# A decode kernel whose last four weight blocks move from behind TensorE's loop into its body

## The chip, the cores and the metric

The kernel runs on one core of one Trainium2 chip. The metric is the device time of one execution in microseconds. Three runs of the kernel before took 775.5, 776.76 and 776.8 us; their median is 776.76 us.

## The reference

Two branches on the same two rows `x` (2 x 1024) are mixed by a gate:

```python
g = sigmoid((x * gate_w).sum(-1, keepdims=True))
q = (x @ wq)                               # 32 heads of 128, 4 kv heads, 32768 cached positions
a = softmax(q k^T / sqrt(128)) v, heads joined, @ wo      # wo: 4096 x 1024
b = x + gelu(layernorm(x) @ w3) @ w4       # w3: 1024 x 3584, w4: 3584 x 1024
out = g * a + (1 - g) * b
```

The sequence has one position, so the shifted branch through `w1` and `w2` is zero and isn't computed. All data are float32. The keys and values (two caches of 2 x 4 x 32768 x 128) are 268 MB of the 331 MB that are read.

## The kernel before, in words

All large data come through one queue, SP's, in one order: `wq`, `w3`, then for each of the 8 pairs of batch row and kv head two halves of 8 MB of keys and two of values, with `w4` between pair 3 and pair 4 and `wo` behind pair 7. They go into two buffers (`ring`, named `load` in the trace) of 64 KB per partition. A load waits until TensorE has finished with what stood in its buffer (`load`, L196), so that while one half is worked on, the other one is under way.

A "block" of `w4` or `wo` is 128 x 1024 numbers, one per partition row: `w4` has 28 blocks, `wo` 32. The first 28 blocks of either go into the two ring buffers in four pieces of 14, 8, 4 and 2 blocks (`weights`, `STEPS`). The last four blocks of `wo` have a buffer of their own, `tail` (16 KB per partition), filled by three loads: two blocks, one block, one block, with the semaphores `came[4]`, `came[5]` and `came[6]`.

TensorE's program has straight code at its start (projections of `wq` and `w3`), then a loop of two passes (L491). One pass runs four turns of an inner loop (L492, `turn`, one pair each) and then `weigh` (L482), which multiplies the 28 blocks by the columns in `w_pad` and adds them to `acc`: in the first pass the blocks are `w4`'s and the columns the activations, in the second pass `wo`'s and the attention outputs. Behind the loop stands straight code for the last four blocks of `wo`, from `tail`, with columns of their own, `o_pad` (L570 to L573):

```python
for sem, cs in ((came[4], (0, 1)), (came[5], (2,)), (came[6], (3,))):
    pe.after((sem, 16))
    for c in cs:
        last = into_acc(o_wide, c, tail[:, c * D:(c + 1) * D], last=(c == 3))
```

`into_acc` (L346) issues 8 matmuls of 32 columns by 128 per block. A float32 matmul stands in the trace as two records on PE and two weight loads on PEld, so a block is 16 records. `Line.take` (L49) is one instruction on the waiting engine that waits for a semaphore and lowers it again, so that a loop can use the same semaphore in each pass; `Line.after` is a plain wait.

VectorE, behind its own loop, waits for the end of the `w4` pass (`weighed(1)`) and writes the gated attention outputs to `o_pad` and `w_pad` (L565), then releases TensorE's second `weigh`. ScalarE copies `acc` out after `END` and issues the output's DMA. GpSimd clears the padded buffers at the start (L259), and VectorE waits for the last of these before it writes the first padded columns (L290).

Of the kernel before, what the change touches and what calls it, by code (L numbers as in the profile page):

```python
# [15 lines left out]
B, D, HQ, HKV, SK, DH, F = 2, 1024, 32, 4, 32768, 128, 3584  # L16
REP = HQ // HKV
PAIRS = B * HKV
# [4 lines left out]
KF = F // P  # L23
C = 32
# [4 lines left out]
SHIFT = 8  # L29
# [42 lines left out]
def kernel(  # L72
# [47 lines left out]
    nc = tc.nc  # L120
# [5 lines left out]
    def new(name, *shape, parts=P):  # L126
        return sb.tile([parts, *shape], F32, name=name)

    ring = [new(f"load{i}", PART, WIDE) for i in range(2)]
    tail = new("tail", 4 * D)  # L130
# [3 lines left out]
    x_pad = new("x_pad", KD, C)  # L134
    xn_pad = new("xn_pad", KD, C)
    xr_wide = new("xr_pad", SHIFT + KD * C)
    q_pad = new("q_pad", PAIRS + 1, PART, 2, C)
    q_cur = new("q_cur", PART, 2, C)
    o_all = new("o_all", PAIRS, PART, REP)
    o_wide = new("o_pad", SHIFT + 4 * C)  # L140
    w_wide = new("w_pad", SHIFT + KF * C)
    xr_pad, o_pad, w_pad = (t[:, SHIFT:].rearrange("p (k c) -> p k c", c=C) for t in (xr_wide, o_wide, w_wide))
    sel = new("sel", G, REP)
    sel_all = new("sel_all", REP)
    part = new("part", 2 * B)
# [1 line left out]
    gate = new("gate", B)  # L147
# [16 lines left out]
    p = new("p", NI, NT, PART + 1, HALF)  # L164
# [19 lines left out]
    pe, dve, act, pool, sp = (Line(tc, e, n) for e, n in (  # L184
        (nc.tensor, "pe"), (nc.vector, "dve"), (nc.scalar, "act"), (nc.gpsimd, "pool"), (nc.sync, "sp")))
    landed = [tc.alloc_semaphore(f"landed{i}") for i in range(2)]
    came = [tc.alloc_semaphore(f"came{i}") for i in range(7)]
# [8 lines left out]
    def load(dst, src, sem, *marks):  # L196
        sp.after(*marks)
        nc.sync.dma_start(dst, src).then_inc(sem, 16)  # L198

    def run(src, j):  # L200
        return src[PART * j:PART * (j + 1)].rearrange("i (q w) c -> (i q) (w c)", w=PART)
# [5 lines left out]
    PROLOGUE = ("run", "sum", "var", "q0", "q1", "qt", "h0", "h1", "ht")  # L207
    TURN = ("k0", "v0", "v1")
    STEP = ("s0", "s2", "s3", "mt", "bp", "tp00", "tp01", "tp02", "tp03", "tp10", "tp11", "tp12", "tp13", "lp", "op")

    def at(name, m=None):
        if m is None:
            return (pe.sem, 1 + PROLOGUE.index(name))
        return (pe.sem, len(PROLOGUE) + m * len(TURN) + m // 4 * 2 + 1 + TURN.index(name))

    def weighed(i):
        return (pe.sem, len(PROLOGUE) + 4 * len(TURN) + 1 + i)

    END = (pe.sem, len(PROLOGUE) + PAIRS * len(TURN) + 2 * 2 + 1)


    load(flat[0], run(wq, 0), came[0])
    load(flat[1], run(wq, 1), came[1])
    sixteen = nc.sync.to_reg(16)
    load(flat[0][:, :PART * 2 * F], run(w3, 0), came[2], at("q0"))
    load(flat[1][:, :PART * 2 * F], run(w3, 1), came[3], at("q1"))

    half = PART * KF // 4
    STEPS = ((0, 14), (14, 8), (22, 4), (26, 2))

    def weights(src, *free):
        for (lo, n), sem in zip(STEPS, w_in):
            j = lo // half
            piece = slice((lo - j * half) * D, (lo - j * half + n) * D)
            load(flat[j][:, piece], run(src, j)[:, piece], sem, free[j])

    for m in range(PAIRS):
        free = [at("h" + "01"[j]) if m == 0 else at("v" + "01"[j], m - 1) for j in range(2)]
        if m == 4:
            weights(w4, *free)  # L240
            free = [weighed(0), weighed(1)]
        for j in range(2):
            load(flat[j], run(kt[m], j), landed[j], free[j])
        for j in range(2):
            load(flat[j], run(vt[m], j), landed[j], (at("k0", m), (k1_free, m + 1))[j])
    weights(wo, at("v0", PAIRS - 1), at("v1", PAIRS - 1))
    load(tail[:, :2 * D], run(wo, 0)[:, half * D:], came[4])
    for c in range(2):
        load(tail[:, (2 + c) * D:(3 + c) * D], run(wo, 1)[:, (half + c) * D:(half + c + 1) * D], came[5 + c])


    nc.scalar.dma_start(xg_sb, xg).then_inc(got_x, 16)
# [2 lines left out]
    made = pool.mark(nc.gpsimd.affine_select(  # L255
        out=ident, in_=ident, pattern=[[-1, P]], base=0, channel_multiplier=1,
        compare_op=ALU.not_equal, fill=1.0))
    for t in (x_pad, xn_pad, xr_wide, q_pad, o_wide, w_wide):
        zeroed = pool.mark(nc.gpsimd.memset(t, 0.0))  # L259
    d_ones = dve.mark(nc.vector.memset(ones, 1.0))  # L260
    dve.after(made)
# [13 lines left out]
    for i in range(2):  # L275
        last = nc.vector.tensor_copy(perm[:, :, i], ident.rearrange("p (q w) -> p w q", w=PART))
    d_perm = dve.mark(last)

    def over_k(t):
# [5 lines left out]
    d_part = dve.mark(nc.vector.tensor_reduce(  # L285
        part[:, B:2 * B], xs.rearrange("p k b -> p b k"), axis=AX.X, op=ALU.add))
    dve.after(at("run"), zeroed)
    for i in range(2):
        own = slice(i * HALF, (i + 1) * HALF)
        last = nc.vector.tensor_copy(  # L290
            x_run[own].rearrange("p (j w k) b -> p j w (k b)", j=2, w=PART),
            tr[1][own, :PART * KD * B].rearrange("p (w j i k b) -> p i j w (k b)", w=PART, j=2, i=2, b=B)[:, i])
# [21 lines left out]
    for w in range(PART):  # L314
        last = nc.tensor.matmul(tr[1][:, w * KD * B:(w + 1) * KD * B], perm[:, w].rearrange("p i q -> p (i q)"), xs,  # L315
                                start=True, stop=True)
# [25 lines left out]
    def shifted(t, k, i):  # L342
        lo = SHIFT * (1 - i) + k * C
        return t[:, lo:lo + C]

    def into_acc(t, k, rows, last=False):  # L346
        for i in range(2):
            for g in range(G):
                lo = (2 * g + i) * P
                inst = nc.tensor.matmul(acc[C * g:C * g + C], shifted(t, k, i), rows[:, lo:lo + P],  # L350
                                        start=False, stop=(last and i == 1), skip_group_check=True)
        return inst
# [11 lines left out]
    for i in range(2):  # L364
        last = nc.vector.tensor_copy(twice[:, :, :, i], row.rearrange("p u (h q w) -> p (u h) w q", q=HALF, w=PART))
# [3 lines left out]
    for r in range(REP):  # L369
        for w in range(PART):  # L370
            last = nc.tensor.matmul(qt_ps[:, w, r], twice[:, r, w].rearrange("p i q -> p (i q)"), compact,
                                    start=True, stop=True)
    done = pe.mark(last)
    dve.after(done)
    for i in range(2):
        own = slice(i * HALF, (i + 1) * HALF)
        for s in range(2):
            lo = (2 * s + i) * REP
            last = nc.vector.tensor_copy(q_pad[own, :PAIRS, :, s, lo:lo + REP], qt_ps[own].rearrange("p w h m -> p m w h"))
# [15 lines left out]
    n = KF // G  # L395
    both = p.rearrange("p i t w q -> p (i t w q)")[:, :n * P * 2].rearrange("p (c w i q) -> p c w i q", c=n, w=PART, i=2)
    dve.after(d_h, a_h, at("qt"))
    for i in range(2):
        last = nc.vector.tensor_copy(
            both[:, :, :, i], row.rearrange("p u n -> p (u n)")[:, :n * P].rearrange("p (c q w) -> p c w q", q=HALF, w=PART))  # L400
# [3 lines left out]
    for c in range(n):  # L404
        for w in range(PART):
            o = (c * PART + w) * PAIRS
            last = nc.tensor.matmul(ht_ps[:, o:o + PAIRS], both[:, c, w].rearrange("p i q -> p (i q)"), compact,
                                    start=True, stop=True)
# [11 lines left out]
    for i in range(2):  # L420
        for j in range(2):
            own = slice(i * HALF, (i + 1) * HALF)
            last = nc.vector.tensor_mul(
                w_pad[own, j * PART * n:(j + 1) * PART * n, ::C // B].rearrange("p (w c) b -> p w c b", w=PART),
                h[own].rearrange("p (c w j i b) -> p i j w c b", c=n, w=PART, j=2, i=2)[:, i, j],
                rest[own].rearrange("p (o z b) -> p o z b", o=1, z=1).to_broadcast([HALF, PART, n, B]))
# [55 lines left out]
    def weigh():  # L482
        pe.take(x_in)
        for (lo, n), sem in zip(STEPS, w_in):
            pe.take(sem, 16)
            for c in range(lo, lo + n):
                last = into_acc(w_wide, c, flat[c // half][:, c % half * D:(c % half + 1) * D])
            if lo == 0 or lo + n == KF:
                pe.mark(last)

    with nc.tensor.Fori(0, 2, 1):  # L491
        with nc.tensor.Fori(0, PAIRS // 2, 1):  # L492
            turn()
        weigh()
# [22 lines left out]
    with nc.vector.Fori(0, PAIRS, 1) as m:  # L517
        turn_of = Turn(dve, own_step)
        for i in range(NI):
            if i != 1:  # L520
                nc.vector.wait_ge(*seen(f"s{i}"))
                if i == 3:
                    nc.vector.sem_inc(k1_free, 1)
                last = [nc.vector.reduce_max(out=mx[:, k:k + 1], in_=sc[k], axis=AX.X)  # L524
                        for k in ((1, 2) if i == 2 else (i,))][-1]
# [19 lines left out]
        for i in range(2):  # L545
            last = nc.vector.tensor_copy(pv_sb[:, :, :, i], pv.rearrange("p (s q w) -> p s w q", q=HALF, w=PART))  # L546
# [9 lines left out]
        dve.take(step, len(STEP))  # L556


    dve.after(weighed(1))
    o_by_block = o_all.rearrange("p (a i b) w h -> p i a (w h) b", a=2, i=2)  # L560
    for t, lo, n in ((o_pad, half, 2), (w_pad, 0, half)):
        for i in range(2):
            own = slice(i * HALF, (i + 1) * HALF)
            for b in range(B):
                last = nc.vector.tensor_scalar_mul(  # L565
                    t[own, :, b * (C // B)].rearrange("p (j c) -> p j c", j=2), o_by_block[own, i, :, lo:lo + n, b],
                    gate[own, b:b + 1])
    last.then_inc(x_in, 1)

    for sem, cs in ((came[4], (0, 1)), (came[5], (2,)), (came[6], (3,))):  # L570
        pe.after((sem, 16))
        for c in cs:
            last = into_acc(o_wide, c, tail[:, c * D:(c + 1) * D], last=(c == 3))  # L573
    last.then_inc(pe.sem, 1)
    act.after(END)
    a_out = act.mark(nc.scalar.copy(o_sb, acc))  # L576
    act.after(a_out)
# [34 lines left out]
```

## Time and profile before

| what | value |
|---|---|
| median of 3 runs | 776.76 us (775.5 to 776.8) |
| the profiled execution's own time | 777.06 us |
| its span, first to last instruction | 775.3 us |
| busy: PE, PEld, DVE, ACT, POOL | 433.7, 198.0, 94.2, 60.7, 3.4 us |
| DMA | 331.53 MB at a mean of 428 GB/s |
| granted TensorE clock, mean | 0.763 |
| last chain, shares of the span | DMA `tail<-wo` 4%, PE `pv` 1% |

The span covers what the engines did; 1.8 us of the execution's time lie outside of it. The page divides the span into 40 equal slices of 19.4 us and gives for each the busy share of an engine or of the 16 DMA engines in tenths. A matmul's start is measured and its end modelled. "PEq L51" as the releaser of idle time is the wait instruction in `take`, mostly for a load; "issue" is idle time in which the engine waited for nothing that the profile shows. "q8 instruction" among the DMA queues carries instructions, not data.

### The profile page before, as it was taken

How to read it: one execution, taken by the hardware profiler on the slowest of the kernel's cores; microseconds unless marked ns; L12 is line 12 of the kernel's file. 1: busy time of each engine (PE TensorE's matmuls, PEld its weight loads, DVE VectorE, ACT ScalarE, POOL GpSimd, SP SyncE). 2: the span in 40 equal slices, each digit the busy share in tenths (PEclk: the TensorE clock that was granted, in tenths of full speed). 3: DMA queues.
4: the chain of work that ended last, by engine and by line, in shares of the span. 5: the costliest groups of instructions: out<-in, count | busy, mean ns of one | idle time of the engine just before them, and what ended most of it. 6: DMA issues, size and time to landing. Idle time of an engine off the chain costs nothing. (4 is left out here: it accounts for less than half of the span.)

```text
span 775.3 us, 8384 instructions
## 1 busy us (share of the span) xinstructions
PE 433.7 (56%) x3772; PEld 198.0 (26%) x3772; DVE 94.2 (12%) x266; ACT 60.7 (8%) x144; POOL 3.4 (0%) x12
## 2 busy tenths in 40 slices
PE   0564747454746564647466247465646474547475
PEld 0231413221323132213235013131312131213164
DVE  1110202100210021002100002100210021002110
ACT  0000002000200020002000002000200020002000
POOL 1000000000000000000000000000000000000000
PEclk9977676876686688677879567767967787768779
DMA  9999999999999999999999999999999999999996
GB/s 379 433 431 437 436 437 440 430 434 436 440 433 436 436 433 433 433 433 433 429 420 446 433 433 433 433 433 433 433 433 433 433 433 436 433 433 433 424 424 265
DMA packets 6955, 331.53 MB, mean 428 GB/s; under 512 B 913, under 2 KB 929, under 8 KB 1185
## 3 DMA queue, kind: packets, MB, share of 16 engines
q1 hardware_dynamic: 6768, 331.35, 99.0%
q8 instruction: 9, 0.15, 0.1%
q10 hardware_dynamic: 176, 0.02, 0.0%
q14 instruction: 2, 0.01, 0.0%
HBM read 331.36 MB, written 0.01 MB: 427 GB/s over the span
## 5 line engine op out<-in xcount | busy, mean ns | idle before, releaser
L441 PE MATMUL sc<-load,q_cur 128*32 128x512 f32 x1024 | 151.2, 756 | 133.1 <-PEq L51 133.1
L468 PE MATMUL pv<-load,pt 128*32 128x512 f32 x1024 | 131.5, 672 | 89.4 <-PEq L51 89.4
L441 PEld LDWEIGHTS sc<-load,q_cur 128*32 128x32 f32 x1024 | 41.3, 135 | 236.6 <-issue 236.6
L468 PEld LDWEIGHTS pv<-load,pt 128*32 128x32 f32 x1024 | 39.7, 122 | 171.4 <-issue 171.4
L458 PE MATMUL sc<-ident,p 128*128 128x128 f32 x256 | 44.4, 347 | 22.8 <-PEq L51 22.8
L524 DVE TENSOR_REDUCE mx<-sc 128x1 f32<-128x512 f32 x32 | 21.4, 689 | 287.8 <-PE sc L441 287.8
L508 ACT ACT_TABLE_LOAD x8 | 10.3, 1283 | 493.6 <-ACTq L51 493.6
L458 PEld LDWEIGHTS sc<-ident,p 128*128 128x128 f32 x256 | 39.9, 183 | 30.0 <-issue 30.0
L350 PE MATMUL acc<-load,w_pad 128*32 128x128 f32 x896 | 30.3, 299 | 13.9 <-PEq L51 10.3
L541 DVE COPY pt<-sc 64x256 f32<-64x256 f32 x64 | 25.9, 414 | 71.9 <-PE sc L458 71.5
L350 PEld LDWEIGHTS acc<-load,w_pad 128*32 128x32 f32 x896 | 28.3, 122 | 15.6 <-issue 15.6
L514 ACT COPY pt<-sc 64x256 f32<-64x256 f32 x64 | 23.5, 368 | 75.9 <-PE sc L458 73.6
L546 DVE COPY pv_sb<-pv 128x512 f32<-128x512 f32 x16 | 10.3, 685 | 152.9 <-PE tr L474 152.9
L478 PE MATMUL tr<-sel,pv_sb 128*128 128x8 f32 x128 | 20.6, 298 | 11.8 <-PEq L51 11.8
L478 PEld LDWEIGHTS tr<-sel,pv_sb 128*128 128x128 f32 x128 | 20.1, 247 | 12.3 <-issue 12.3
L330 PE MATMUL sc<-load,x_pad 128*32 128x512 f32 x128 | 17.4, 706 | 7.5 <-DMA load<-wq 7.5
L508 ACT ACTIVATE p<-sc,bias 128x512 f32<-128x512 f32 x32 | 21.6, 686 | 0.1
L330 PE MATMUL sc<-load,xn_pad 128*32 128x384 f32 (+1 forms) x128 | 15.1, 631 | 11.3 <-DMA load<-w 11.3
L315 PE MATMUL tr<-xg_sb,perm 128*128 128x16 f32 x4 | 1.0, 372 | 23.4 <-DMA xg_sb<-xg 23.4
L537 DVE COPY p<-p 128x256 f32<-128x256 f32 x32 | 9.4, 294 | 26.7 <-ACT p L508 26.7
L330 PEld LDWEIGHTS sc<-load,xn_pad 128*32 128x32 f32 x128 | 4.2, 126 | 21.9 <-DMA load<-w 12.4
L330 PEld LDWEIGHTS sc<-load,x_pad 128*32 128x32 f32 x128 | 4.3, 128 | 19.8 <-issue 11.3
(83 smaller groups left out, 88.7 us busy)
## 6 DMA issues: line engine op xcount, KB each, us to landing
load<-w SPq DMA_DIRECT2D x3, 7168.0 KB, 26.2
load<-wo SPq DMA_DIRECT2D x1, 7168.0 KB, 28.6
load<-w SPq DMA_DIRECT2D x1, 4096.0 KB, 17.6
load<-wo SPq DMA_DIRECT2D x1, 4096.0 KB, 17.0
load<-w SPq DMA_DIRECT2D x1, 2048.0 KB, 22.2
load<-wo SPq DMA_DIRECT2D x1, 2048.0 KB, 21.6
load<-w SPq DMA_DIRECT2D x1, 1024.0 KB, 24.1
load<-wo SPq DMA_DIRECT2D x1, 1024.0 KB, 23.6
```

The costliest lines, as they stand in the source:

```text
L330: last = nc.tensor.matmul(b[C * g:C * g + C, :hi - lo], pad[:, k], t[:, o + lo:o + hi], start=(k == 0), stop=(k == KD - 1))
L350: inst = nc.tensor.matmul(acc[C * g:C * g + C], shifted(t, k, i), rows[:, lo:lo + P], start=False, stop=(last and i == 1), skip_group_chec ...
L441: last = nc.tensor.matmul(sc[i][C * g:C * g + C], q_cur[:, w, s], ring[j][:, w, o:o + 512], start=(s == 0 and w == 0), stop=(s == 1 and w ...
L458: last = nc.tensor.transpose(sc[k][:, t * P:(t + 1) * P], pair.rearrange("p w q -> p (w q)"), ident)
L468: last = nc.tensor.matmul(pv[C * g:C * g + C], pt[j][w][:, lo:lo + C], ring[j][:, w, o:o + G * DH], start=(j == 0 and w == 0 and t == 0), ...
L478: last = nc.tensor.matmul(tr[1][:, w * REP:(w + 1) * REP], pv_sb[:, s, w].rearrange("p i q -> p (i q)"), sel[:, s], start=(s == 0), stop=( ...
L508: nc.scalar.activation(p[:, i, :, :PART], sc[i].rearrange("p (t q w) -> p t w q", t=NT, w=PART), AF.Exp, bias=bias, scale=scale, accum_out ...
L514: nc.scalar.copy(*halves(1, j, c)).then_inc(pt_in[c], 1)
L524: last = [nc.vector.reduce_max(out=mx[:, k:k + 1], in_=sc[k], axis=AX.X) for k in ((1, 2) if i == 2 else (i,))][-1]
L537: nc.vector.tensor_copy(p[:, i, :, PART], p[:, i, :, 0]).then_inc(p_in[i], 1)
L541: nc.vector.tensor_copy(*halves(0, j, c)).then_inc(pt_in[c], 1)
L546: last = nc.vector.tensor_copy(pv_sb[:, :, :, i], pv.rearrange("p (s q w) -> p s w q", q=HALF, w=PART))
```

## The change

The three parts for `tail` move into `weigh`, and so into the loop's body. They now run in both passes. In the first one they multiply zeros by zeros: GpSimd clears `tail` at the start, and the columns 28 to 31 of `w_pad` stay zero until VectorE writes them after the first pass. `o_pad` goes; `w_pad` grows from 28 to 32 blocks of columns. So that the first pass doesn't wait for loads, VectorE raises the three semaphores by 16 each at the start, and `take` lowers them again. `pe.mark` behind the last block is a third mark per pass (the `* 2` in `at` becomes `* 3`), VectorE waits for this third mark (`weighed(2)`) before it writes `w_pad`, and ScalarE's `END` is the same mark in the second pass.

```diff
-    o_wide = new("o_pad", SHIFT + 4 * C)
-    w_wide = new("w_pad", SHIFT + KF * C)
+    w_wide = new("w_pad", SHIFT + HQ * C)
...
-        return (pe.sem, len(PROLOGUE) + m * len(TURN) + m // 4 * 2 + 1 + TURN.index(name))
+        return (pe.sem, len(PROLOGUE) + m * len(TURN) + m // 4 * 3 + 1 + TURN.index(name))
...
-    END = (pe.sem, len(PROLOGUE) + PAIRS * len(TURN) + 2 * 2 + 1)
+    END = (pe.sem, len(PROLOGUE) + PAIRS * len(TURN) + 2 * 3)
...
-    for t in (x_pad, xn_pad, xr_wide, q_pad, o_wide, w_wide):
+    for t in (x_pad, xn_pad, xr_wide, q_pad, w_wide, tail):
         zeroed = pool.mark(nc.gpsimd.memset(t, 0.0))
...
     dve.after(at("run"), zeroed)
+    for sem in came[4:]:
+        nc.vector.sem_inc(sem, 16)
...
             if lo == 0 or lo + n == KF:
                 pe.mark(last)
+        lo = 0
+        for (_, _, n), sem in zip(rest_of_wo, came[4:]):
+            pe.take(sem, 16)
+            for c in range(lo, lo + n):
+                last = into_acc(w_wide, KF + c, tail[:, c * D:(c + 1) * D], last=(c == 3))
+            lo += n
+        pe.mark(last)
...
-    dve.after(weighed(1))
+    dve.after(weighed(2))
...
-    for t, lo, n in ((o_pad, half, 2), (w_pad, 0, half)):
+    for c, lo, n in ((0, 0, half), (KF, half, 2)):
...
-    for sem, cs in ((came[4], (0, 1)), (came[5], (2,)), (came[6], (3,))):
-        pe.after((sem, 16))
-        for c in cs:
-            last = into_acc(o_wide, c, tail[:, c * D:(c + 1) * D], last=(c == 3))
-    last.then_inc(pe.sem, 1)
```

The loads themselves, their order and the buffers that they wait for stay as they are.

On TensorE the program's end, before. L441 to L478 are the inner loop's turn, the branch at L492 closes it, the branch at L491 closes the outer loop, and the number behind x counts matmuls:

```order
L441 MATMUL sc_104<-load_61,q_cur 32x512 x16
L441 MATMUL sc_105<-load_61,q_cur 32x512 x16
...
L468 MATMUL pv<-load_62,pt 32x512 x32
L474 MATMUL tr_108<-lsel,ones 128x8
L478 MATMUL tr_109<-sel,pv_sb 128x8 x8
L492 COMPARE_AND_BRANCH
L350 MATMUL acc<-load_61,w_pad 32x128 x112
L350 MATMUL acc<-load_62,w_pad 32x128 x112
L491 COMPARE_AND_BRANCH
L350 MATMUL acc<-tail,o_pad 32x128 x32
```

And of the change:

```order
L471 MATMUL pv<-load_62,pt 32x512 x32
L477 MATMUL tr_107<-lsel,ones 128x8
L481 MATMUL tr_108<-sel,pv_sb 128x8 x8
L502 COMPARE_AND_BRANCH
L353 MATMUL acc<-load_61,w_pad 32x128 x112
L353 MATMUL acc<-load_62,w_pad 32x128 x112
L353 MATMUL acc<-tail,w_pad 32x128 x32
L501 COMPARE_AND_BRANCH
```

The 32 matmuls on `tail` stood behind the outer loop's branch and now stand ahead of it.

On GpSimd the clearing at the start, before:

```order
L259 MEMSET xn_pad 128x256
L259 MEMSET xr_pad 128x264
L259 MEMSET q_pad 128x1152
L259 MEMSET o_pad 128x136
L259 MEMSET w_pad 128x904
```

And of the change:

```order
L260 MEMSET xn_pad 128x256
L260 MEMSET xr_pad 128x264
L260 MEMSET q_pad 128x1152
L260 MEMSET w_pad 128x1032
L260 MEMSET tail 128x4096
```

The small `o_pad` went, `w_pad` grew by 128 elements per partition, and `tail` with 4096 came behind all others.

## Rows read from the trace of the kernel before

**Rows 1.** The page: the span, then DMA busy tenths and GB/s in 40 slices.
```profile
span 775.3 us, 8384 instructions
DMA  9999999999999999999999999999999999999996
GB/s 379 433 431 437 436 437 440 430 434 436 440 433 436 436 433 433 433 433 433 429 420 446 433 433 433 433 433 433 433 433 433 433 433 436 433 433 433 424 424 265
```

**Rows 2.** The chain that ended last, its end: start us, us, what.
```profile
742.85 28.58 DMA tail<-wo
...
771.47 0.69 PE acc L350 x16
```

**Rows 3.** Timeline at the end: start us, us, engine, line, what, count, idle before and its releaser.
```profile
765.14 1.08 PE L350 MATMUL acc<-load,w_pad 128*32 128x128 f32 x32 [0.53 <-PEq L51]
767.56 1.86 PE L350 MATMUL acc<-tail,o_pad 128*32 128x128 f32 x48 [1.33 <-DMA tail<-wo]
768.78 0.38 PEld L350 LDWEIGHTS acc<-tail,o_pad 128*32 128x32 f32 x16 [0.41 <-DMA tail<-wo]
771.47 0.64 PE L350 MATMUL acc<-tail,o_pad 128*32 128x128 f32 x16 [2.05 <-DMA tail<-wo]
```

**Rows 4.** Windows at the end: stretch, length, busy us of five engines, PEclk, DMA share, GB/s.
```profile
768.00:769.00 1.00, 0.86 (x32) 0.59 (x28) 0.00 (x0) 0.00 (x0) 0.00 (x0) 1.00 0.54 221
...
769.60:770.20 0.60, 0.00 (x0) 0.00 (x0) 0.00 (x0) 0.00 (x0) 0.00 (x0) 1.00 0.00 0
770.20:771.02 0.82, 0.00 (x0) 0.00 (x0) 0.00 (x0) 0.00 (x0) 0.00 (x0) 1.00 0.06 10
```

**Rows 5.** DMA queue of instructions, whole span: packets, MB, share of 16 engines.
```profile
q8 instruction: 9, 0.15, 0.1%
```

**Rows 6.** The same queue in the stretch 0 to 90 us.
```profile
q8 instruction: 2, 0.03, 0.1%
```

**Rows 7.** The same queue in the stretch 90 to 165 us.
```profile
q8 instruction: 3, 0.05, 0.3%
```

**Rows 8.** The same queue in the stretch 405 to 426 us.
```profile
q8 instruction: 3, 0.05, 1.0%
```

**Rows 9.** The same queue in the stretch 768 to 771 us.
```profile
q8 instruction: 1, 0.02, 2.3%
```

**Rows 10.** Timeline of PE alone, the w4 pass and the next turn's start (that group's first four).
```profile
404.43 7.47 PE L350 MATMUL acc<-load,w_pad 128*32 128x128 f32 x199 [4.38 <-PEq L51]
412.75 0.93 PE L350 MATMUL acc<-load,w_pad 128*32 128x128 f32 x25 [0.86 <-issue]
414.15 3.04 PE L350 MATMUL acc<-load,w_pad 128*32 128x128 f32 x103 [0.47 <-PEq L51]
420.00 3.57 PE L350 MATMUL acc<-load,w_pad 128*32 128x128 f32 x121 [2.81 <-issue]
440.86 1.08 PE L441 MATMUL sc<-load,q_cur 128*32 128x512 f32 x4 [17.28 <-PEq L51]
```

**Rows 11.** The page's group of transposes in all eight turns: busy, mean ns, idle before.
```profile
L458 PE MATMUL sc<-ident,p 128*128 128x128 f32 x256 | 44.4, 347 | 22.8 <-PEq L51 22.8
```

**Rows 12.** Timeline of PE where loads land early in the program (the third line cut at 80 us).
```profile
42.48 8.98 PE L330 MATMUL sc<-load,x_pad 128*32 128x512 f32 x64 [7.54 <-DMA load<-wq]
60.80 7.51 PE L330 MATMUL sc<-load,xn_pad 128*32 128x512 f32 x64 [1.87 <-DMA load<-w]
77.73 2.57 PE L330 MATMUL sc<-load,xn_pad 128*32 128x512 f32 x12 [9.43 <-DMA load<-w]
97.18 8.94 PE L441 MATMUL sc<-load,q_cur 128*32 128x512 f32 x64 [2.80 <-PEq L51]
```

**Rows 13.** Timeline of PE at the last pair's second half of values (cut at 732 us).
```profile
731.11 1.93 PE L468 MATMUL pv<-load,pt 128*32 128x512 f32 x8 [9.97 <-PEq L51]
```

**Rows 14.** Timeline at the start: GpSimd's last clearing, VectorE's first padded columns.
```profile
3.53 0.85 POOL L259 MEMSET w_pad<- 128x904 f32 x1
24.46 0.36 DVE L290 COPY x_run<-tr 64x16 f32<-64x16 f32 x2 [0.69 <-PE tr L315]
```

More of the change, by code (lines that the diff above doesn't have):

```diff
@@ L139 @@
     o_all = new("o_all", PAIRS, PART, REP)
-    o_wide = new("o_pad", SHIFT + 4 * C)
-    w_wide = new("w_pad", SHIFT + KF * C)
-    xr_pad, o_pad, w_pad = (t[:, SHIFT:].rearrange("p (k c) -> p k c", c=C) for t in (xr_wide, o_wide, w_wide))
+    w_wide = new("w_pad", SHIFT + HQ * C)
+    xr_pad, w_pad = (t[:, SHIFT:].rearrange("p (k c) -> p k c", c=C) for t in (xr_wide, w_wide))
     sel = new("sel", G, REP)
@@ L246 @@
     weights(wo, at("v0", PAIRS - 1), at("v1", PAIRS - 1))
-    load(tail[:, :2 * D], run(wo, 0)[:, half * D:], came[4])
-    for c in range(2):
-        load(tail[:, (2 + c) * D:(3 + c) * D], run(wo, 1)[:, (half + c) * D:(half + c + 1) * D], came[5 + c])
+    rest_of_wo = [(run(wo, 0), 0, 2), (run(wo, 1), 0, 1), (run(wo, 1), 1, 1)]
+    lo = 0
+    for (src, c, n), sem in zip(rest_of_wo, came[4:]):
+        load(tail[:, lo * D:(lo + n) * D], src[:, (half + c) * D:(half + c + n) * D], sem)
+        lo += n
     nc.scalar.dma_start(xg_sb, xg).then_inc(got_x, 16)
@@ L489, in weigh @@
                 pe.mark(last)
+        lo = 0
+        for (_, _, n), sem in zip(rest_of_wo, came[4:]):
+            pe.take(sem, 16)
+            for c in range(lo, lo + n):
+                last = into_acc(w_wide, KF + c, tail[:, c * D:(c + 1) * D], last=(c == 3))
+            lo += n
+        pe.mark(last)
     with nc.tensor.Fori(0, 2, 1):
@@ L565 @@
                 last = nc.vector.tensor_scalar_mul(
-                    t[own, :, b * (C // B)].rearrange("p (j c) -> p j c", j=2), o_by_block[own, i, :, lo:lo + n, b],
-                    gate[own, b:b + 1])
+                    w_pad[own, c:c + 2 * n, b * (C // B)].rearrange("p (j c) -> p j c", j=2),
+                    o_by_block[own, i, :, lo:lo + n, b], gate[own, b:b + 1])
     last.then_inc(x_in, 1)
-    for sem, cs in ((came[4], (0, 1)), (came[5], (2,)), (came[6], (3,))):
-        pe.after((sem, 16))
-        for c in cs:
-            last = into_acc(o_wide, c, tail[:, c * D:(c + 1) * D], last=(c == 3))
-    last.then_inc(pe.sem, 1)
     act.after(END)
```

## The prediction

> **What bounds the kernel now.** I read the page first. The DMA row shows 9 in every slice but the last and 420 to 446 GB/s in slices 2 to 38 [rows 1]: the transfers never pause, so all compute before the end is cover, and only two things can move the time, how much the transfers carry and what happens after the last of them. The chain of waits confirms it: its last 28.58 us are the transfer into `tail`, and behind it stand 0.69 us of TensorE [rows 2].
>
> The second place is the end itself, in the timeline. The three loads of `tail` release TensorE at 767.56, 768.78 and 771.47 us [rows 3]. What should they be apart? From 440.86 us [rows 10] to 731.11 us [rows 13] TensorE was released by 15 loads of 8 MB later: 290.25 / 15 = 19.35 us each. The last two loads have 0.5 MB, 1.21 us each. The second one keeps this (767.56 + 1.21 = 768.77). The third is due at 769.99 and comes at 771.47, 1.48 us late. The windows say what is in that gap: the DMA engines run empty, 0.54 of them busy in 768 to 769, none of the data queues in 769.6 to 770.2, and then one of sixteen (0.06) until 771.0 [rows 4]. One engine is late and all others are done. In that stretch there is one packet of the instruction queue [rows 9]. So the kernel ends on one DMA engine that fetched instructions in front of the last data. That is what the change touches: the code that ran there for the first time would now have run before.
>
> **When instructions are fetched.** There are 9 packets of 0.15 MB in all, some 16 KB each [rows 5]: 2 until 90 us, 3 until 165, 3 in the first pass over `w4`, 1 at the end [rows 6 to 9], which leaves none for anywhere else. So jumping back in a loop cost no fetch, neither in the inner loop's turns nor when the outer loop went back near 424 us. In the `w4` pass TensorE stood still twice for no reason that the profile shows, 0.86 and 2.81 us. Between the restarts lie 25 + 103 = 128 matmul records [rows 10]; each has a weight load, so that is 256 instructions, and 16 KB is one such block at 64 bytes each. The stalls are entries into blocks that had not arrived. Of the pass's 448 records, 199 shown (200 by its weight loads) and 128 stood before the second stall, some 120 follow it: the next block begins about 8 records, or a few less for the waits and branches, behind the pass. In the program before that is in the first block on `tail`. TensorE enters it at 767.6 us and the ninth fetch follows at once, although all 64 records on `tail` end before another block: a fetch is for the block behind the one that is entered. I read from this that entering a block fetches the next one.
>
> **Which engine pays.** The projections show what one fetch costs the loads. From 42.48 to 60.80 us lies one 7 MB load, 18.32 us, where 7/8 of 19.35, 16.93, was due: 1.39 us late, with the first fetch in it. The next interval is 16.93 again and then 19.45 for 8 MB [rows 12]. From 97.18 to 440.86 us pass 16 loads of 8 MB and 14 MB of `w4`, 17.75 x 19.35 = 343.46 us; it took 343.68. So the first fetch made the last engine's share of each load 1.4 us later for good, the next seven added 0.2 us together, and the ninth again added 1.48. Seven that cost nothing must have gone to engines that were not late; the ninth went to one that was already among the last. I take it that eight places with an engine each are used in turn, and that the ninth block takes the place and the engine of the first one fetched.
>
> **The change part by part.**
> - The ninth fetch moves, it does not go. In the first pass the 64 records now run on past the `w4` pass and enter the same block near 424 us. The delayed engine stays late: no pause follows in which it could catch up [rows 1]. Price: minus 1.48 at the end, plus 1.39 to 1.48 from there on, so 0.
> - The outer loop goes back from a block farther. A turn has 138 float32 matmuls of two records and 33 transposes (16 + 16 + 1) of one, as 256 for 8 turns show [rows 11]: 309. With 448 that is 757 records, 1,514 instructions, with some 40 waits and branches about 1,555 up to the boundary, a little over 6 blocks. So the loop before touched 7 blocks and had the eighth fetched ahead, and all stayed. The new loop touches 8 and has a ninth fetched ahead, in the place of the block with the loop's head. What happens then the trace cannot show. Lower bound 0 (nothing displaced). Upper bound: the head is fetched again by the late engine, and when the second pass enters the last block the one behind it, displaced in turn, is fetched once more, in front of the last data as now: two more fetches on the late engine, 2 x 1.39 to 2 x 1.48 = 2.8 to 3.0 us. I take the upper one, 2.9, since the seven cheap fetches and the dear ninth speak for eight places.
> - If the loop's other blocks are fetched again too, their engines become late by one more fetch, less than the engine above. TensorE would stall in the `wo` pass as it did in `w4`'s, 0.86 + 2.81 = 3.7 us. It ended that pass at 766.2; with all of it 769.9, and the four blocks take 1.86 + 0.64 = 2.5 us [rows 3], 772.4, ahead of a last load near 774.4. Covered; without that cover, with one more stall of 2.8, the end is 1 us later, which goes into the range.
> - The four blocks in the first pass, 2.5 us of TensorE, and a wait of a few us for their code lie in the 17.28 us that it then waits for keys [rows 10]. Without that cover they would delay the release of buffers.
> - Clearing `tail`: 904 elements took 0.85 us, 4096 then 3.9, ending near 8.3 us; VectorE needs it at 24.46 [rows 14]. Cost 0. Three semaphore increments on VectorE ahead of that copy: between 0 and three times half of the two copies' 0.36, 0.5 us. They delay the first projection, behind which TensorE waits 7.54 us for `wq` [rows 12]. Cost 0.
> - At the end `take` stands for a plain wait, one instruction for one, and VectorE writes the same eight pieces. Within 0.1 us either way.
>
> Sum: the profiled execution's 777.06 + 2.9 = 779.96, so 780.0; the median of the runs shown lies 0.30 lower, so 779.6 us is the forecast.
>
> [...]
>
> **The rivals.**
> - Not slower: the store holds a ninth block, or keeps the loop's head. For it: nothing in the trace shows a block being lost. Against it: the engine of the ninth fetch. The fetch then only moves to an engine that stays late, 777.06 + 0, or 776.8 as a median. It decides at one block more than eight.
> - Faster: the delayed engine makes up its 1.48 us in the 340 us after the first pass, or the ninth block falls to an engine that isn't late: 777.06 - 1.48 = 775.6, as a median 775.3. Against it: after the first fetch no interval was short by 1.4 us, up to 440 us. A gain of 1.48 us is 0.19%.
> - Blocks are fetched again, but by engines in turn, so that the second fetch of the head goes to one that is late once, and only a full refill comes round to the late one: 0.1 to 1.5 us more, 776.9 to 778.3.
> - That the edit does nothing can be left out: the order of the instructions shows the 32 matmuls ahead of the branch.
>
> **How the numbers follow.** Forecast (two more fetches on the late engine) 0.48; not slower 0.27; other engines 0.19; faster 0.06. About 0.2%, 1.55 us, is what a measurement can tell from no change. Slower by more: the forecast and a third of the third case, which reaches that mark only at its upper end, 0.54. Faster by more: 0.04, since even the whole gain is 0.19%. The same: 0.42. The forecast's own range is 779.0 to 780.8, with 1 us for the stall above. To hold 8 in 10 the range must take in the rival at 776.8 and its scatter: 776.2 to 780.8; the faster case is left out.
>
> **What would show it.** Right: 11 or more instruction packets instead of 9, at least one of them between 426 and 740 us, one again behind 768 us; the third load of `tail` landing near 774.4 us, with a longer stretch in which one or two of sixteen DMA engines run. In the first pass a third idle stretch of TensorE, just ahead of or inside the blocks on `tail`. Wrong: 9 packets with none at the end. If the last load then lands near 771.4 us, the late engine stayed late; if near 770.0, it caught up, and my account of the lag is wrong.

## The result: 0.4% slower, with the profile after

The changed kernel takes 779.4 us as the median of 6 runs (779.04 to 780.28), the kernel before 776.78 us (6 runs). The ratio is 1.004 with a 95% interval of 1.0027 to 1.0053. The profiled execution took 779.42 us, 2.36 more than that of before.

The page of the changed kernel, the span, the DMA rows and the instruction queue (packets, MB, share of 16 engines):

```profile
span 777.6 us, 8520 instructions
DMA  9999999999999999999999999999999999999995
GB/s 378 435 435 450 442 432 432 432 429 435 432 432 432 432 432 432 432 435 432 429 434 431 434 432 436 429 432 432 432 435 432 438 432 442 432 432 432 434 410 238
q8 instruction: 18, 0.29, 0.2%
```

The DMA view of the same kernel for 431 to 520 us:

```profile
q8 instruction: 6, 0.10, 0.4%
```

And for 750 to 777 us:

```profile
q8 instruction: 4, 0.07, 1.0%
```

The transfers run as evenly as before [rows 1], but there are 18 instruction packets where there were 9 [rows 5]. Before there was none between 426 and 765 us. Now the eighth comes at 426.30 us, six come behind the first pass over the blocks (the ninth and, by their number, five that fetch again), and four in the second pass over them.

TensorE's timeline in the first pass (start, us, engine, line, what, count, idle before and its releaser), to set beside [rows 10]:

```profile
404.34 7.40 PE L353 MATMUL acc<-load,w_pad 128*32 128x128 f32 x199 [4.44 <-PEq L51]
412.82 0.92 PE L353 MATMUL acc<-load,w_pad 128*32 128x128 f32 x25 [1.08 <-issue]
414.05 3.04 PE L353 MATMUL acc<-load,w_pad 128*32 128x128 f32 x103 [0.30 <-PEq L51]
420.46 5.24 PE L353 MATMUL acc<-load,w_pad 128*32 128x128 f32 x121 [3.36 <-issue]
425.43 0.39 PE L353 MATMUL acc<-tail,w_pad 128*32 128x128 f32 x5
428.64 3.48 PE L353 MATMUL acc<-tail,w_pad 128*32 128x128 f32 x59 [2.83 <-issue]
442.20 1.94 PE L444 MATMUL sc<-load,q_cur 128*32 128x512 f32 x8 [10.07 <-PEq L51]
444.66 8.31 PE L444 MATMUL sc<-load,q_cur 128*32 128x512 f32 x56 [0.53 <-issue]
```

The third stall stands five records into the four blocks, where the block boundary was read from the rows of before. The next turn's keys release TensorE at 442.20 instead of 440.86 us: one DMA engine has become 1.34 us later. And TensorE stalls again, for 0.53 us until 444.66, eight records into the turn: code that had been run four times is waited for.

The chain that ended last (start, us, what):

```profile
759.20 0.04 issue
759.24 3.04 PE acc L353 x103
762.28 3.09 issue
765.37 5.36 PE acc L353 x126
770.73 0.90 issue
771.63 2.04 PE acc L353 x59
773.66 0.02 issue
773.69 0.27 ACT o_sb L581
```

Before, this chain was the transfer into `tail` [rows 2]. Now the profile draws no transfer in it: from 759 us on TensorE runs its matmuls and waits twice for its own instructions, 3.09 and 0.90 us. The windows put the last data ahead of the last block; from 772.6 us on nothing moves (stretch, length, busy us of five engines, PEclk, DMA share, GB/s):

```profile
771.00:772.00 1.00, 0.37 (x16) 0.37 (x19) 0.00 (x0) 0.00 (x0) 0.00 (x0) 1.00 0.07 29
772.00:772.60 0.60, 0.60 (x32) 0.60 (x24) 0.00 (x0) 0.00 (x0) 0.00 (x0) 1.00 0.03 14
772.60:773.66 1.06, 1.03 (x31) 0.66 (x23) 0.00 (x0) 0.00 (x0) 0.00 (x0) 1.00 0.00 0
```

The output's DMA in the DMA view of before, the last number issue to landing in us:

```profile
out<-o_sb ACTq DMA_DIRECT2D x1, 8.0 KB, 1.7
```

And of the change:

```profile
out<-o_sb ACTq DMA_DIRECT2D x1, 8.0 KB, 2.5
```

So the 2.3 us of span have two parts: TensorE's last record ends 1.50 us later (773.66 against 771.47 + 0.69), and the output lands 0.8 us slower. In the stretch from 772 to 777 us, which holds the output, there is one packet of the instruction queue, from 774.50 to 775.45 us; the output's own packets ran from 775.22 to 775.51.

The chain shows what ended last, not by how much. A load raises its semaphore in sixteen steps, and the trace records the time of each; I take each step for one of the 16 DMA engines. For the last load of `tail`:

| kernel | code packets ahead of the last data | times of the sixteen steps, us |
|---|---|---|
| experiment 11, below | 7 | nine at 767.85 to 769.08, seven at 769.46 to 769.82 |
| before | 9 | eight at 767.90 to 768.96, seven at 769.38 to 769.94, one at 771.43 |
| the change | 17 | eight at 767.78 to 769.26, seven at 771.01 to 771.43, one at 772.85 |

Seven packets make seven steps late by some 1.5 us. Nine make eight late, one of them twice. Seventeen make seven late twice and one three times. That fits eight engines that fetch code in turn, each some 1.5 us later for every fetch. So the change's last load came in at 772.85 us, 1.42 later than before, and TensorE's wait for it (`take`, L51) was done right behind, at 772.88. In experiment 12, which leaves that load out, the same wait was done at 771.81, 0.51 us behind TensorE's last restart instead of 1.25. The waits of `take` on TensorE's queue (count, shortest, median and longest in ns, first and last start in us), in the change:

```profile
L51 PEldq EVENT_SEMAPHORE  x184: 51/51/51, 89.4 to 772.9; - x184
```

And in experiment 12:

```profile
L51 PEldq EVENT_SEMAPHORE  x184: 51/51/51, 91.4 to 771.8; - x184
```

So TensorE did wait for the late load as well; the chain has no piece for it. It cost little: the last 59 records took 2.04 us in the change and 1.95 in experiment 12. The stalls and the late load end within 0.1 us of each other, so either one alone would have brought nearly all of the 1.50 us (an estimate from this one execution).

### The profile page after: what moved, and what is told of

Its sections match the earlier page's. It is cut to its first block, busy times and chain, and to the rows that moved or that the text cites. A ratio compares the mean times of both kernels' runs of the same rounds, so it can differ in the third digit from the quotient of the medians.

```text
span 777.6 us, 8520 instructions
## 1 busy us (share of the span) xinstructions
PE 435.4 (56%) x3836; PEld 198.5 (26%) x3836; DVE 93.3 (12%) x266; ACT 60.7 (8%) x144; POOL 7.0 (1%) x12
## 5 line engine op out<-in xcount | busy, mean ns | idle before, releaser
L444 PE MATMUL sc<-load,q_cur 128*32 128x512 f32 x1024 | 149.0, 746 | 130.3 <-PEq L51 129.8
L353 PE MATMUL acc<-load,w_pad 128*32 128x128 f32 x896 | 33.0, 315 | 18.6 <-PEq L51 9.7
L353 PEld LDWEIGHTS acc<-load,w_pad 128*32 128x32 f32 x896 | 30.8, 128 | 20.4 <-issue 20.2
L481 PE MATMUL tr<-sel,pv_sb 128*128 128x8 f32 x128 | 18.5, 281 | 11.8 <-PEq L51 11.8
L333 PE MATMUL sc<-load,xn_pad 128*32 128x384 f32 (+1 forms) x128 | 16.7, 687 | 9.6 <-DMA load<-w 9.6
L481 PEld LDWEIGHTS tr<-sel,pv_sb 128*128 128x128 f32 x128 | 18.0, 225 | 12.3 <-issue 12.3
```

Of the source, the lines that this page charges most:

```text
L333: last = nc.tensor.matmul(b[C * g:C * g + C, :hi - lo], pad[:, k], t[:, o + lo:o + hi], start=(k == 0), stop=(k == KD - 1))
L444: last = nc.tensor.matmul(sc[i][C * g:C * g + C], q_cur[:, w, s], ring[j][:, w, o:o + 512], start=(s == 0 and w == 0), stop=(s == 1 and w ...
L481: last = nc.tensor.matmul(tr[1][:, w * REP:(w + 1) * REP], pv_sb[:, s, w].rearrange("p i q -> p (i q)"), sel[:, s], start=(s == 0), stop=( ...
```

## The experiments

Three theories. **A**, reach: TensorE holds eight blocks of 256 instructions (256 from the 128 records between two stalls [rows 10], eight an estimate from seven fetches that cost 0.2 us together and a ninth that cost 1.48); a loop that touches eight and has a ninth fetched ahead loses its head and is fetched anew. **B**, place: the four blocks, their zeros, waits and marks cost where they now stand. **C**, catching up: a DMA engine that has become late makes it up again. The first group only shifts the program against the block boundaries, by matmuls of four instructions each at its start, where TensorE waits for `x`: ten in experiments 1 and 3, four in 2, one in 4.

```diff
+    pe.after(d_ones)
+    for _ in range(10):
+        nc.tensor.matmul(pv[:, :1], ones, ones[:, :1], start=True, stop=True)
     pe.after(d_perm, (got_x, 16))
```

**Experiment 1, the change with 40 instructions more.**

> The changed kernel with ten small matmuls (40 instructions) added at the start of TensorE's program, while it waits for x; they only shift where the 256-instruction blocks begin. Theory A (the loop no longer fits: it touches eight blocks and has a ninth fetched ahead, so the loop's head is displaced and all is fetched again): shifted by 40, the loop touches seven blocks and the eighth is fetched ahead, all stays. 9 instruction packets, none after 440 us, time as the kernel before, 776.8 within 0.5 us; the saved fetch at the end gives nothing because the ninth fetch goes to an engine that is late already and stays late. Theory B (it is the code's place that costs: the waits, the third mark, the zero blocks in the first pass): 779.4 stays. Theory C (a late engine catches up): 775.3.

Measured: 777.0 us, ratio to before 1.0003 (0.9994 to 1.0012), 9 packets. The loss is gone with all of the change in place. TensorE at the end:

```profile
766.22 1.08 PE L356 MATMUL acc<-load,w_pad 128*32 128x128 f32 x32 [0.54 <-PEq L51]
768.70 1.86 PE L356 MATMUL acc<-tail,w_pad 128*32 128x128 f32 x48 [1.40 <-PEq L51]
771.16 0.64 PE L356 MATMUL acc<-tail,w_pad 128*32 128x128 f32 x16 [0.60 <-PEq L51]
```

No stall on instructions is left in the second pass, and the queue has one packet between 426 and 440 us and none after. Still the last load releases TensorE only at 771.16. Its pieces come 1.1 us later than in [rows 3], 766.22 against 765.14, as did the first keys behind the first pass, 441.87 against 440.86 [rows 10]: an engine is late from the first pass on and has not caught up at the end. That is why moving the fetch gains nothing; theory C falls.

**Experiments 2 to 4, the kernel before with 16, 40 and 4 instructions more.**

> The kernel before with four small matmuls (16 instructions) at the same place. Nothing of the change is in it. Theory A: the boundary that lay some ten instructions behind the loop's end now lies some six ahead of it, the loop's head is still in the same block, so the loop touches eight blocks and a ninth is fetched: some 18 instruction packets, TensorE stalled again in the wo pass, 778.5 to 779.8. Theory B: 776.8, 9 packets.

> The kernel before with ten small matmuls (40 instructions) at the same place. Theory A: the loop's head falls into the next block, the loop touches seven, everything stays; the ninth fetch now comes in the w4 pass and none at the end, 9 packets. With a late engine that stays late the last load still lands near 771.4 and the time is 776.8 within 0.4 us. Theory C (the engine catches up, or the ninth goes to another engine): the last load lands near 770.0, 775.3 us.

> The kernel before with one small matmul (4 instructions) at the same place, the control for added instructions as such. Theory A: the boundary stays behind the loop's end: 9 packets, one of them at the end, 776.8 within 0.3 us. If added instructions cost by themselves: more than before, and less than with 16 or 40.

Measured: 776.96 (ratio 1.0004, 0.9995 to 1.0013), 777.08 (1.0005, 0.9996 to 1.0014) and 776.85 us (0.9999, 0.999 to 1.0008); 9 packets each, the last of them at the end. The control, 4, is as expected. Experiment 2 is a miss for theory A, and 3 in its account of the ninth packet. In experiment 3 TensorE did stall on entering the block, 14 records ahead of the pass's end:

```profile
421.51 0.81 PE L353 MATMUL acc<-load,w_pad 128*32 128x128 f32 x18 [0.27 <-PEq L51]
423.93 0.65 PE L353 MATMUL acc<-load,w_pad 128*32 128x128 f32 x14 [1.60 <-issue]
```

So it entered the block and ran some 29 instructions of it, but the next block was not fetched until the second pass. Entering is not what fetches; some way into the block is.

**Experiments 5 and 6, 64 dead instructions in the loop.** The dead matmuls write into `acc`'s bank with a start flag, and the output of both is off by a relative error of 0.50; what in them does it is not shown.

```diff
             if lo == 0 or lo + n == KF:
                 pe.mark(last)
+        for _ in range(16):
+            nc.tensor.matmul(acc_bank[:C, 2 * P:3 * P], ones[:, :C], ones, start=True, stop=True)
```

> The kernel before with 16 dead matmuls (64 instructions, into columns of acc's bank that nobody reads) at the end of the loop's pass; the four wo blocks stay behind the loop. Experiment 2 had entered the last block by some six instructions and no fetch followed, so the fetch of the next block comes only some way into a block, between about 30 and 120 instructions. Theory A with this correction: 54 instructions in, the ninth fetch comes in the first pass, the loop's head is displaced, some 18 instruction packets, TensorE stalled in the wo pass, 778.3 to 779.8 us. Theory B (the place of the wo blocks costs): 9 packets, 776.9.

> The same with 40 more instructions (ten small matmuls) at the program's start, where TensorE waits for x. Theory A: the loop's head falls into the next block, the longer loop touches seven, all stays: 9 packets, the ninth in the first pass, none at the end, 776.9 within 0.4 us, although this program is the longest of all. If the length of the loop cost by itself: as experiment 5 or more.

Measured: 776.77 us (ratio 1.0002, 0.9993 to 1.0011) with no packet between 426 and 440 us, a second miss; and 777.68 us (1.0013, 1.0004 to 1.0022) with one packet there and none later. By my count, good to a few instructions, experiment 5 goes 54 instructions into the block and experiment 6 goes 94: the fetch of the next block comes between the two. The time of experiment 6 is 0.4 us above its range because 31 dead records, all for one row group, took 3.55 us (64 spread over the row groups took 1.96 in experiment 10) and pushed the last blocks, not because anything was fetched twice.

**Experiments 9 and 10, 128 dead instructions in the loop**, as many as the change adds, spread over the row groups of a bank that is free there:

```diff
+        for j in range(32):
+            lo = j % G * C
+            nc.tensor.matmul(pv[lo:lo + C, :P], ones[:, :C], ones, start=True, stop=True)
```

> The kernel before with 32 dead matmuls (128 instructions, into the pv bank, which is free there) at the end of the loop's pass, as many as the change puts there; wo's four blocks stay behind the loop and nothing else of the change is in it. Experiments 1 to 6 put the fetch of the next block between 54 and 94 instructions into a block; here the loop goes 119 into its last one. Theory A: as the change, 18 instruction packets, fetched again after 426 us, TensorE stalled in the wo pass until about 771.6 us; behind that stand 59 dead and 64 real records at 34 ns, 4.2 us instead of the change's 2.0, so 780.5 to 782. Theory B (the real blocks, their waits or their zeros cost): 9 packets, 777.

> The same with 40 more instructions at the program's start. Theory A: the loop touches seven blocks again, the ninth fetch is in the first pass, all stays: 9 packets (a tenth only behind the last matmul), the dead matmuls run where TensorE waited for the last loads, 777.0 within 0.5. If the dead matmuls cost by themselves: as experiment 9.

Measured: 780.66 us (ratio 1.0049, 1.0035 to 1.0063) with 18 packets, and 776.77 us (1.0, 0.9991 to 1.0009) with 10, the tenth at 771.21 us, behind the last data. The instruction queue over the whole span, in experiment 9:

```profile
q8 instruction: 18, 0.29, 0.2%
```

And in experiment 10:

```profile
q8 instruction: 10, 0.16, 0.1%
```

This settles it for theory A: the kernel before, with wo's blocks where they were and nothing of the change in it, loses in the change's way from 128 dead instructions, and 40 more at the start take the loss away. It loses more than the change, 3.7 against 2.6 us, because the dead and the real records stand behind the last stall, 3.70 us (772.82 to 776.52) against 2.04. The chain of experiment 9 has the stalls of the change:

```profile
763.63 3.09 issue
766.72 3.57 PE acc L350 x121
770.29 0.13 PE pv L492 x6
770.42 2.41 issue
772.82 1.82 PE pv L492 x57
```

**Experiment 12, which of two ends sets the time.** The kernel leaves out the last block of `wo`.

```diff
+        if sem is not came[6]:
             load(tail[:, lo * D:(lo + n) * D], src[:, (half + c) * D:(half + c + n) * D], sem)
...
-        nc.vector.sem_inc(sem, 16)
+        nc.vector.sem_inc(sem, 32 if sem is came[6] else 16)
```

> The changed kernel without the last load of 0.5 MB (the last block of wo is left out; its buffer keeps its zeros, and VectorE raises that semaphore for both passes at the start). It parts the two things that end the changed kernel together. If TensorE's wait for its own instructions sets the end, the last load is cover and the time stays: 779.3 within 0.4. If the late DMA engine sets it, the data are there 1.2 us earlier: 778.2. If both matter alike: between.

Measured: 779.03 us (778.25 to 780.09), ratio 1.0033 (1.002 to 1.0045). Most of the loss stays without the last 1.2 us of transfer, and the chain is the same as in the change:

```profile
762.14 2.81 issue
764.96 5.36 PE acc L354 x126
770.31 0.99 issue
771.30 1.95 PE acc L354 x59
```

So TensorE's waits for its instructions are enough for most of the loss by themselves: the data that are left were in at 771.54 us, 1.31 earlier than in the change, and TensorE ended at 773.26, only 0.40 earlier. The late engine is not ruled out by this: the change's TensorE waited for it too, and by the estimate above it would have brought almost the same end; no run has the fetches without the stalls. The runs scatter by 1.8 us: three took 778.25 to 778.54 us, three 779.51 to 780.09. The profiled one is the fastest, 1.17 us under the change's. Beside the 0.40 it has a faster output, 1.8 instead of 2.5 us; its last code packet was over at 773.90, ahead of the output's packets at 774.80. What the slower three did no profile shows.

**Experiments 7, 8 and 11, a shorter program.**

```diff
-        for i in range(2):
-            for g in range(G):
-                lo = (2 * g + i) * P
-                inst = nc.tensor.matmul(acc[C * g:C * g + C], shifted(t, k, i), rows[:, lo:lo + P],
-                                        start=False, stop=(last and i == 1), skip_group_check=True)
+        for g in range(G):
+            lo = 2 * g * P
+            inst = nc.tensor.matmul(acc[C * g:C * g + C], shifted(t, k, 0), rows[:, lo:lo + 2 * P],
+                                    start=False, stop=last, skip_group_check=True)
```

In 7 and 8 both matmuls that open a row group of `acc` carry the start flag, and the output of both is off by a relative error of 0.67; in 11 the first one alone carries it, and the output is whole.

> The kernel before with a block of w4 or wo multiplied in four matmuls of 256 columns instead of eight of 128 (acc and the output are 256 wide): TensorE's program is 512 instructions shorter, two blocks. Theory A: 7 instruction packets instead of 9, none after 430 us, all to different engines; the last load lands near 770.0 instead of 771.4, and the last block takes 0.4 instead of 0.7 us: 775.2 us (774.8 to 775.5). If the engine were late at the end for another reason than the ninth fetch: 776.5.

> The changed kernel with the same four matmuls per block: the blocks of wo are in the loop as in the change, and the loop is 512 instructions shorter. Theory A: 7 packets, nothing fetched again, the time of experiment 7, 775.2 us within 0.3. Theory B (the place of the wo blocks in the loop costs 2.6 us): 777.5 or more.

> Experiment 7 with the start flag set on the first of the two matmuls that open a row group of acc, and not on the second, so that the first one's result is kept. No instruction more or less: 7 packets, none after 430 us, 775.6 us within 0.3.

Measured: 775.64 us (ratio 0.9992, 0.9983 to 1.0001), 775.67 (0.9987, 0.9978 to 0.9996) and 775.64 (0.9987, 0.9978 to 0.9996), 7 packets each. Experiments 7 and 8 differ in the change alone, and their times are the same: the place of the four blocks costs nothing that the runs can tell when the loop fits. TensorE at the end of experiment 11:

```profile
767.40 1.07 PE L349 MATMUL acc<-tail,o_pad 128*32 128x256 f32 x16 [1.33 <-DMA tail<-wo]
768.64 0.64 PE L349 MATMUL acc<-tail,o_pad 128*32 128x256 f32 x8 [0.17 <-DMA tail<-wo]
769.87 0.64 PE L349 MATMUL acc<-tail,o_pad 128*32 128x256 f32 x8 [0.59 <-DMA tail<-wo]
```

The last two releases are 1.23 us apart, where [rows 3] had 2.69. The last block still takes 0.64 us, not the 0.4 that I expected, and the wider copy (0.37 against 0.27 us) gives a little back; by the medians 1.2 to 1.3 us are left of the 1.5. Experiment 11 is the fastest version found.

## Why the prediction was right, and where it was not

- **Direction, size and cause.** Forecast 779.6 us, measured 779.4: the loop's head is displaced and its code fetched again. Experiments 1, 9 and 10 show it. The sum behind the number did not come out. The first rival's "store" is the eight places, and their number is an estimate: it rests on the seven fetches without cost and the ninth with 1.48 us, and no run shows it by itself. Experiments 9 and 10 fit it: by the count of blocks in the prediction, seven and one ahead stay, and one more brings 18 packets. At the crossings of blocks TensorE waited up to 3.09 us in this chain.
- **"The ninth fetch moves, it does not go", price 0: right.** In experiment 1 the last load releases TensorE at 771.16 us although nothing is fetched after 440 us.
- **"Two more fetches on the late engine, 2.8 to 3.0 us": wrong, it was one more, 1.42 us.** I let the displaced head go back to its own place and engine. Not two blocks are fetched again but nine (18 packets against 9): as I read it, each one that comes back displaces the next, so that the engines are gone through in turn. Their turn, which I had assumed, fits the sixteen steps, and by it the late engine has the 1st, the 9th and the 17th packet; the 17th ran from 769.17 us, ahead of the last data. The last load landed at 772.85 us instead of some 774.4. The last load did end the chain together with the stalls, as the release at 772.88 shows. For the loads this is my third rival, a full refill that comes round to the late engine, at its upper end of 1.5 us; that rival lacked the stalls and the output.
- **"Covered", the step on TensorE's stalls: failed.** I added 0.86 and 2.81 us to an end of 766.2 and left a margin of some 2 us. The pass started 1.18 us later (749.52 against 748.34 in the trace of before; experiment 1, with one engine late since the first pass, has 749.41), and the stalls were 1.32, 3.09 and 0.90 us, in part in place of waits for loads. TensorE ended at 773.66 instead of 772.4, and the load that should have covered it was in 1.5 us earlier than I had it. The margin came out as 0.1 us.
- **The output: missing from the sum.** It took 2.5 instead of 1.7 us. This is the one trace in which a code packet overlaps it; in experiments 9, 10 and 12, whose last packet was over before, it took 1.7, 1.7 and 1.8 us. That the packet is the cause rests on this comparison.
- **"Entering a block fetches the next one": too simple.** By my count the fetch comes after 54 and before 95 instructions of a block (experiments 5 and 6). The change goes 121 into its last block, so this made no difference to it, but it did to experiments 2, 3 and 5.
- **What cost nothing, as said:** clearing `tail` took 3.51 us and ended at 7.9 us; VectorE's copy came at 24.73 instead of 24.46 us, behind which TensorE still waited 5.78 us for `wq`.

That 2.9 and the measured 2.36 us lie close is luck. The loop was displaced and fetched again as forecast, but the one term of the sum was twice what it measured, and the output and the stalls, which were not in it, gave back 0.9 us of what it missed.

## What to carry to other kernels

Count a loop on TensorE in instruction blocks, from where its head lies to where its end lies plus the one fetched ahead: here 40 more instructions at the start took the whole loss away, 777.0 us instead of 779.4. Here, where the transfers never paused, a fetch of code made a DMA engine late up to the end, by some 1.5 us each, so that a shorter program gained though no compute engine's work was on the path: four matmuls of 256 columns for eight of 128 saved two fetches and 1.2 to 1.3 us. And when one chain ends last, ask how far behind it the next one ends: here taking away the last load alone gave back only 0.4 us of TensorE's 1.50.

## What was not expected of the hardware

The ninth fetch of the kernel before does not always fall in front of the last data. Experiment 3's profiled execution took 775.62 us where its median is 777.08. Its ninth packet is at the end as well, but the last load releases TensorE on time, 1.21 us behind the one before:

```profile
768.81 0.65 PE L353 MATMUL acc<-tail,o_pad 128*32 128x128 f32 x16 [0.18 <-DMA tail<-wo]
770.02 0.64 PE L353 MATMUL acc<-tail,o_pad 128*32 128x128 f32 x16 [0.57 <-DMA tail<-wo]
```

All sixteen steps of that load are in by 769.98 us. Its ninth packet started at 769.07, the one in the trace of before at 769.16; what decides between the two stays open. Of the 33 executions of the kernel before beside experiments 1 to 4, four took 775.4 to 775.8 us and the others 776.6 to 777.4. I take the four for executions like this one, but none of them was profiled. With 7 packets all 11 executions of experiment 11 lie between 775.57 and 776.32 us.
